# Attention probabilities that pass through HBM: four stores and two loads by key chunks in place of one store and four loads, and one product moved behind the others

## The chip, the cores and the metric

The kernel runs on one core of a Trainium2 chip. The metric is the device time of one execution in microseconds (us). TensorE (PE, with its weight loads PEld), VectorE (DVE), ScalarE (ACT) and GpSimd (POOL) each work through their own instruction list in order; SyncE (SP) issues the DMA transfers in order and waits, where an instruction must wait, at that place.

## The reference

Decayed causal attention over 32 heads (4 batches of 8), 576 queries and keys of width 64, then two dense layers of two matrices each over all 2304 tokens:

```python
scores = scale * np.matmul(q, k.transpose(0, 1, 3, 2))
decay = cum[:, :, :, None] - cum[:, :, None, :]
scores = np.where(causal, -1000000000.0, scores + decay)
attn = np.exp(scores - np.max(scores, axis=-1, keepdims=True))
attn = attn / (np.sum(attn, axis=-1, keepdims=True) + 1e-09)
out = np.matmul(attn, v)                  # per head
h = np.maximum(x @ w_in, 0.0); x = h * h @ w_out
h = x @ w_in2; out = (h - np.tanh(h)) @ w_out2
```

## The kernel before

Every product that needs fp32 accuracy is made from operands split into a rounded high part and a rest, so a product becomes two or three matmuls. PE makes the scores of a head (`s_ps`, L476 and L477), the value products (`o_ps`, L549, L552, L554), and in between the products of the first dense layer: twelve matmuls of 288 columns into `hp` (L138) and twelve into `yp` (L164) for each slice of the layer. The work of attention and of the dense layer is interleaved on PE so that one fills the waits of the other. Attention ends at about 550 us of 1080; behind it only dense work is left.

The softmax of a head is made with queries on the partitions, in five query tiles `t` (0 is the first 64 queries, 1 to 4 are 128 each). The value products need the probabilities with keys on the partitions. Heads 8 to 15 are turned by PE transposes (`trans`). Heads 16 to 31, which this change is about, go another way:

- `turn`: DVE transposes 32x32 blocks of the normalised probabilities `P` into the tile `T` (`PT["t"]`), after each query tile; the last of them is the one of t = 0 (L503).
- `put` (L512): one DMA of 1 MB stores `T` to the HBM scratch `p_d`, of which there are two, used in turn.
- `get` (L518): four DMAs load `p_d` into `PTl` (`PT["l"]`), one for each group of 32 partitions. There is one `PTl`, so the load of a head can't start before the value products of the head before it have read it.
- `split_p`: for each of four chunks of 128 keys, POOL makes the high part `PTh` (L90) and DVE the rest, in place in `PTl` (L101).
- `pv`: eight chunk products in the order high 0, high 1, rest 1, high 2, rest 2, high 3, rest 3, rest 0 (L552), the product of the last 64 keys (L549) ahead of the last of them, and `o0`, the product of the first 64 queries (L554), into a PSUM bank of its own. Its operand is the unsplit fourth chunk of `PTl`.

`attention_late` writes a head's steps down in the order scores, turns, `put(k)`, `pv(k-1)`, `get(k)`. Where each engine runs them is not this order: up to block 2 of the dense layer the order of a first build is kept (`MARK`), behind it a scheduler places every instruction by its own model of times. So a change of the transfers also moves instructions on all engines.

Of the kernel before, what the change touches and what calls it, by code (L numbers as in the profile page):

```python
# [9 lines left out]
F32 = mybir.dt.float32  # L10
# [43 lines left out]
def kernel(  # L54
# [10 lines left out]
    nc = tc.nc  # L65
# [8 lines left out]
    p_d = [dram.tile([128, 2048], F32, name=f"p_d{a}") for a in range(2)]  # L74
# [5 lines left out]
    def pre(u):  # L80
        return "" if u < UT else "l_"

    def by(name):
        return {"A": nc.scalar, "V": nc.vector, "P": nc.gpsimd, "S": nc.sync}[ENG[name]]

    def rounded(eng, out, in_):
        if eng is nc.scalar:
            eng.activation(out, in_, AF.Copy)  # L88
        elif eng is nc.gpsimd:
            eng.tensor_scalar(out, in_, 1.0, 1.0, ALU.mult, ALU.mult)  # L90
        else:
            eng.tensor_copy(out, in_)
# [83 lines left out]
    R, QA, QB, VR, VH, ST, XS, P, PT = {}, {}, {}, {}, {}, {}, {}, {}, {}  # L176

    def latest(engine):
        return next(x for x in reversed(nc.cur_bb.bb.instructions) if x.engine == engine)
# [249 lines left out]
    def store_x(b, pair, xs, c0, c1):  # L429
        STORED.add((b, pair, c1))  # L430
        n = c1 - c0
        xh = one.tile([128, S], F32R, tag="xsh", name="xsh")
        rounded(by(pre(b * H) + "xh"), xh[:, :n], xs[:, c0:c1])
        rest(by(pre(b * H) + "xl"), xs[:, c0:c1], xs[:, c0:c1], xh[:, :n])
        nc.sync.dma_start(x_d[b][pair][:, 0, c0:c1], xh[:, :n].bitcast(F32))
        nc.sync.dma_start(x_d[b][pair][:, 1, c0:c1], xs[:, c0:c1])
# [28 lines left out]
    def bank(u, name):  # L465
        return psa.tile([128, 512], F32, tag="at", name=name)
# [42 lines left out]
            nc.vector.transpose(T[:, 0:2, 2, 0], p[:, 512:576].rearrange("p (b j) -> p b j", b=2))  # L509

    def put(u):
        by("put").dma_start(p_d[u % 2], PT["t"].rearrange("p b a s j -> p (b a s j)"))  # L512

    def get(u):
        src = p_d[u % 2].rearrange("(q i) (b n) -> i q b n", q=4, b=4)
        for b in range(4):
            dst = PT["l"][32 * b:32 * b + 32].rearrange("p q a s j -> p q (a s j)")
            by("get").dma_start(dst.bitcast(F32), src[:, :, b])  # L518

    def split_p(a):  # L520
        hi, lo = PT["h"], PT["l"]
# [5 lines left out]
    def pv(u):  # L527
        vh, vr = VH.pop(u), VR.pop(u)
        b, h = divmod(u, H)
        e = h % 2  # L530
        ps = bank(u, "o_ps")
        if u < UT:
            hi, lo = (PT[k].rearrange("p q a s j -> p (q a s j)").rearrange("p (c t j) -> p c t j", c=4, t=4) for k in "hl")
            po = ps.rearrange("p (s j) -> p s j", s=4)
            at = lambda p, c, t: p[:, c, t:]
            po4, p4 = ps[0:64, 384:512].rearrange("p (q j) -> p q j", q=4), PT["t"][0:64, :, 3, 1]
            po_at = lambda t: po[:, t:]
            p0 = PT["t"][0:64, 2:4, 3, 0]
        else:
            hi, lo = PT["h"], PT["l"]  # L540
            po = ps.rearrange("p (q s j) -> p q s j", q=4, s=4)
            at = lambda p, c, t: p[:, :, c, t:]
            po4, p4 = po[0:64, :, 3], lo[0:64, :, 2, 0].bitcast(F32)
            po_at = lambda t: po[:, :, t:]
            p0 = lo[0:64, 0:2, 3, 0].bitcast(F32)
        seq = [(hi, 0), (hi, 1), (lo, 1), (hi, 2), (lo, 2), (hi, 3), (lo, 3), (None, 4), (lo, 0)]
        for n, (pt, c) in enumerate(seq):
            if pt is None:
                nc.tensor.matmul(po4, vr[0:64, 4], p4, start=False, stop=False)  # L549
                continue  # L550
            t = max(0, c - 1)
            nc.tensor.matmul(po_at(t), vh[:, c].rearrange("p a d -> p (a d)"), at(pt, c, t), start=(n == 0), stop=(n == 8))  # L552
        ps0 = bank(u, "o0_ps")
        nc.tensor.matmul(ps0[0:64, 0:64], vr[0:64, 0], p0, start=True, stop=True)  # L554
        if e == 0:
            XS[0] = two.tile([128, S], F32, tag="xs", name="xs")
        xs = XS[0]
        r = slice(64 * e, 64 * e + 64)
        xt = one.tile([64, 512], F32, tag="xsh", name="xt")
        rounded(nc.scalar, xt, ps[64:128])  # L560
        if u < UT:
            nc.vector.tensor_tensor(xs[r, 64:], ps[0:64], xt, ALU.add)
        else:
            nc.vector.tensor_tensor(
                xs[r, 64:].rearrange("p (s q j) -> p q s j", s=4, q=4),
                ps[0:64].rearrange("p (q s j) -> p q s j", q=4, s=4),
                xt.rearrange("p (q s j) -> p q s j", q=4, s=4), ALU.add,
            )
        rounded(by(pre(u) + "xs0"), xs[r, 0:64], ps0[0:64, 0:64])
        if e == 1:  # L570
            store_x(b, h // 2, xs, 0, S)
# [11 lines left out]
    def attention(u0):  # L583
        for p in range(u0 - 2, UT):
            if u0 - 1 <= p:
                load_v(p + 1)
            for t in (1, 4, 3, 2):
                if p >= u0:
                    trans(p, t)
                    yield  # L590
                if u0 <= p + 1:
                    scores(p + 1, t)
                    if t == 1:
                        scores(p + 1, 0)
                    elif p + 1 == UT:
                        turn(t)
                    yield
                if t == 4 and p + 2 < NU:
                    prep(p + 2)
                if t == 3 and p >= u0:  # L600
                    prep_v(p)
            if p + 3 < NU:
                load(p + 3)
            if p >= u0:
                pv(p)
            if p + 1 == UT:
                turn(1)
                turn(0)
                put(UT)
                get(UT)  # L610
            if p >= u0:
                yield

    def attention_late():
        for k in range(UT + 1, NU + 1):
# [25 lines left out]
            if now:  # L641
                turn(1)
                turn(0)
                put(k)
            pv(k - 1)
            yield
            if now:
                get(k)
# [120 lines left out]
    for g in range(len(BLK) * NF + LAG):  # L769
        j, i = divmod(g, NF)  # L770
        if (j, i) == MARK:
            first_part = {x.name for x in nc.cur_bb.bb.instructions}
        if j < len(BLK):
            ph, _, n = BLK[j]
# [23 lines left out]
        if jy >= 0:  # L798
            ph, tok, n = BLK[jy]
# [73 lines left out]
```

## Time and profile before

| | |
|---|---|
| median of 3 runs | 1085.09 us (1083.98 to 1085.87) |
| profiled execution, its own time | 1081.43 us |
| its span, first to last instruction | 1079.7 us |
| PE busy | 1029.2 us, 95% of the span |
| DVE, ACT, POOL busy | 594.0, 524.7, 250.6 us |
| DMA, mean rate over the span | 125 GB/s |

PE is the engine with the least idle time, so the end moves when PE's idle time or its clock does. Idle time of another engine counts only where PE waits for it.

### The profile page before, as it was taken

How to read it: one execution, taken by the hardware profiler on the slowest of the kernel's cores; microseconds unless marked ns; L12 is line 12 of the kernel's file. 1: busy time of each engine (PE TensorE's matmuls, PEld its weight loads, DVE VectorE, ACT ScalarE, POOL GpSimd, SP SyncE). 2: the span in 40 equal slices, each digit the busy share in tenths (PEclk: the TensorE clock that was granted, in tenths of full speed). 3: DMA queues.
4: the chain of work that ended last, by engine and by line, in shares of the span. 5: the costliest groups of instructions: out<-in, count | busy, mean ns of one | idle time of the engine just before them, and what ended most of it. 6: DMA issues, size and time to landing. Idle time of an engine off the chain costs nothing.

```text
span 1079.7 us, 16821 instructions
## 1 busy us (share of the span) xinstructions
PE 1029.2 (95%) x6048; PEld 898.8 (83%) x6048; DVE 594.0 (55%) x1566; ACT 524.7 (49%) x1221; POOL 250.6 (23%) x358
## 2 busy tenths in 40 slices
PE   4899999999999898999999999999999999999998
PEld 3577678888998888888889999888888888888898
DVE  5887777768787767877525545642222322222232
ACT  6977677665556446455436667432222222222232
POOL 4244455555353442534210000000000000000000
PEclk9989999999999899999989999999999999999999
DMA  7657643225955658745646088100200300110010
GB/s 243 199 138 213 185 140 136 89 82 174 293 180 171 195 154 253 258 141 162 184 161 228 2 305 285 45 1 25 92 1 1 117 1 1 39 40 1 1 40 21
DMA packets 63301, 134.83 MB, mean 125 GB/s; under 512 B 6416, under 2 KB 31568, under 8 KB 61168
## 3 DMA queue, kind: packets, MB, share of 16 engines
q1 hardware_dynamic: 63216, 133.74, 38.9%
q8 instruction: 48, 0.79, 0.3%
q14 instruction: 37, 0.30, 0.1%
HBM read 93.94 MB, written 39.78 MB: 124 GB/s over the span
## 4 chain that ended last, share of the span: by engine, by line
PE 75%; DMA 11%; DVE 6%; POOL 2%; issue 2%; SPq 2%; ACT 2%; POOLq 0%; ACTq 0%; DVEq 0%
PE hp L138 32%; PE yp L164 32%; DMA PTl<-p_d 6%; PE o_ps L552 3%; DMA p_d<-T 3%; PE o_ps L367 2%; DVE PTl L101 2%; PE s_ps L476 1%; SPq L518 1%; DVE P L443 1%; PE s_ps L477 1%; DMA raw<-in_w_dram 1%; POOL PTh L90 1%; PE s_ps L326 1%; PE t_ps L487 1%
## 5 line engine op out<-in xcount | busy, mean ns | idle before, releaser
L138 PE MATMUL hp<-xhl,w 128*128 128x288 f32 (+2 forms) x2496 | 454.2, 329 | 2.5 <-ACT tmp L148 1.7
L138 PEld LDWEIGHTS hp<-xhl,w 128*128 128x128 f32 x2496 | 388.8, 192 | 41.0 <-issue 2.7
L164 PE MATMUL yp<-ghl,w 128*128 128x512 f32 (+1 forms) x960 | 216.0, 374 | 0.0
L164 PE MATMUL yp<-gh,w 128*128 128x288 f32 x1024 | 200.9, 301 | 0.0
L164 PEld LDWEIGHTS yp<-ghl,w 128*128 128x128 f32 x960 | 168.4, 188 | 34.5
L153 DVE TENSOR_TENSOR tmp<-hp,tmp 128x512 f32<-128x512 f32 (+1 forms) x80 | 51.0, 638 | 209.8 <-ACT tmp L152 209.8
L164 PEld LDWEIGHTS yp<-gh,w 128*128 128x128 f32 x1024 | 161.9, 191 | 1.6 <-issue 0.4
L152 ACT ACTIVATE tmp<-hp 128x512 f32<-128x512 f32 (+1 forms) x80 | 44.4, 555 | 225.0 <-PE hp L138 224.8
L164 PE MATMUL yp<-gl,w 128*128 128x288 f32 x512 | 133.5, 299 | 2.6 <-DVE gl L101 1.5
L148 ACT ACTIVATE tmp<-hp 128x288 f32<-128x288 f32 x128 | 51.9, 407 | 121.6 <-PE hp L138 118.4
L452 ACT ACTIVATE P<-P,ST 128x320 f32<-128x320 f32 (+4 forms) x151 | 84.6, 561 | 39.5 <-DVE ST L443 38.2
L164 PEld LDWEIGHTS yp<-gl,w 128*128 128x128 f32 x512 | 90.4, 190 | 5.0 <-DVE gl L101 2.3
L463 POOL TENSOR_SCALAR P<-P,ST 128x448 f32<-128x448 f32 (+4 forms) x88 | 58.4, 666 | 93.3 <-DVE ST L457 52.3
L101 DVE TENSOR_TENSOR ghl<-tmp,ghl 128x512 fp32r<-128x512 f32 (+1 forms) x80 | 51.1, 639 | 49.2 <-ACT ghl L88 49.2
L443 DVE CUSTOM_DVE_ANT_0 P<-s_ps,mk 128x320 f32<-128x320 f32 (+3 forms) x151 | 63.6, 433 | 25.2 <-PE s_ps L477 12.0
L101 DVE TENSOR_TENSOR gl<-tmp,gh 128x288 fp32r<-128x288 f32 x96 | 48.4, 505 | 47.2 <-ACT tmp L150 46.6
L101 DVE TENSOR_TENSOR PTl<-PTl,PTh 128x512 fp32r<-128x512 f32 (+1 forms) x64 | 51.9, 841 | 39.4 <-POOL PTh L90 39.3
L88 ACT ACTIVATE ghl<-tmp 128x512 fp32r<-128x512 f32 (+1 forms) x80 | 47.2, 590 | 49.9 <-DVE tmp L153 49.8
L101 DVE TENSOR_TENSOR w<-wst,w 128x512 fp32r<-128x512 f32 x64 | 46.1, 725 | 28.9 <-ACT w L88 28.6
L90 POOL TENSOR_SCALAR PTh<-PTl 128x512 fp32r<-128x512 f32 (+1 forms) x64 | 46.3, 750 | 59.8 <-DMA PTl<-p_d 59.0
L149 ACT ACTIVATE gh<-tmp 128x288 fp32r<-128x288 f32 x128 | 56.5, 443 | 4.1 <-PE yp L164 1.2
L150 ACT ACTIVATE tmp<-tmp 128x288 f32<-128x288 f32 x128 | 56.0, 438 | 2.1
(122 smaller groups left out, 1187.7 us busy)
## 6 DMA issues: line engine op xcount, KB each, us to landing
raw<-in_w_dram SPq DMA_DIRECT2D x64, 512.0 KB
p_d<-T SPq DMA_DIRECT2D x16, 1024.0 KB
PTl<-p_d SPq DMA_DIRECT2D x64, 256.0 KB
R<-in_qk_dram SPq DMA_DIRECT2D x24, 576.0 KB
xhl<-y_d SPq DMA_DIRECT2D x16, 512.0 KB
xhl<-x_d SPq DMA_DIRECT2D x14, 576.0 KB
y_d<-yst SPq DMA_DIRECT2D x14, 576.0 KB
VR<-in_v_dram SPq DMA_DIRECT2D x32, 160.0 KB
```

The costliest lines, as they stand in the source:

```text
L88: eng.activation(out, in_, AF.Copy)
L90: eng.tensor_scalar(out, in_, 1.0, 1.0, ALU.mult, ALU.mult)
L101: eng.tensor_tensor(out, in_, hi.bitcast(F32), ALU.subtract)
L138: nc.tensor.matmul(ps, w[:, k * 128:(k + 1) * 128], xk, start=(jj == 0), stop=(jj == 11))
L148: nc.scalar.activation(tmp, ps, AF.Relu)
L149: nc.scalar.activation(gh, tmp, AF.Square)
L150: nc.scalar.activation(tmp, tmp, AF.Square)
L153: nc.vector.tensor_tensor(tmp, ps, tmp, ALU.subtract)
L164: nc.tensor.matmul(yp[m][:, :n], w[:, c], x, start=(i == 0 and j == 0), stop=(i == NF - 1 and j == 2))
L443: nc.vector.tensor_tensor_reduce(p[:rows, a:b], ps[:rows, :b - a], mk[:rows, o:o + b - a], -0.125, 3.0e38 if mn is None else mn, ALU.add, ...
L452: nc.scalar.activation(p[:rows, :n], p[:rows, :n], AF.Exp, bias=mn, scale=-1.0, accum_out=st[:rows, 1, t:t + 1])
L463: by(n_by).tensor_scalar(p[:rows, :n], p[:rows, :n], st[:rows, 3, t:t + 1], 1.0, ALU.mult, ALU.mult)
```

## The change

The one store becomes four, one for each group of 32 partitions of `T` (`q`), each with four runs of 512 values in a partition. The four loads become two; each fills all 128 partitions, the first with key chunks 0 and 1, the second with chunks 2 and 3, in runs of 256 values. The scratch in HBM keeps its layout. In `pv`, for all of heads 8 to 31, the product `o0` is tied behind the last chunk product on PE.

```diff
     def put(u):
-        by("put").dma_start(p_d[u % 2], PT["t"].rearrange("p b a s j -> p (b a s j)"))
+        dst = p_d[u % 2].rearrange("(b i) (q n) -> i q b n", b=4, q=4)
+        for q in range(4):
+            src = PT["t"][32 * q:32 * q + 32].rearrange("p b a s j -> p b (a s j)")
+            by("put").dma_start(dst[:, q], src)
 
     def get(u):
-        src = p_d[u % 2].rearrange("(q i) (b n) -> i q b n", q=4, b=4)
-        for b in range(4):
-            dst = PT["l"][32 * b:32 * b + 32].rearrange("p q a s j -> p q (a s j)")
-            by("get").dma_start(dst.bitcast(F32), src[:, :, b])
+        src = p_d[u % 2].rearrange("p (q a n) -> p q a n", q=4, a=4)
+        dst = PT["l"].rearrange("p q a s j -> p q a (s j)")
+        for a in (0, 2):
+            by("get").dma_start(dst[:, :, a:a + 2].bitcast(F32), src[:, :, a:a + 2])
...
         ps0 = bank(u, "o0_ps")
-        nc.tensor.matmul(ps0[0:64, 0:64], vr[0:64, 0], p0, start=True, stop=True)
+        with tc.issue_after(latest(EngineType.PE)):
+            nc.tensor.matmul(ps0[0:64, 0:64], vr[0:64, 0], p0, start=True, stop=True)
```

POOL's list at the high parts of head 25, with the semaphores that each instruction waits for (DMAHW0 to DMAHW7 are those of transfers). Before:

```order
L90 TENSOR_SCALAR PTh<-PTl 128x4x128 [waits DMAHW3_49,DMAHW2_49,DMAHW4_49,DMAHW1_49,Pool_49]
L90 TENSOR_SCALAR PTh<-PTl 128x4x128 [waits Pool_49]
L90 TENSOR_SCALAR PTh<-PTl 128x4x96 [waits Pool_49]
L90 TENSOR_SCALAR PTh<-PTl 128x4x64 [waits Pool_49]
L463 TENSOR_SCALAR P_1551<-P_1551,ST 128x448 [waits DVE_49,Activation_49]
```

And the same place in the changed kernel:

```order
L90 TENSOR_SCALAR PTh<-PTl 128x4x128 [waits DMAHW5_49]
L90 TENSOR_SCALAR PTh<-PTl 128x4x128
L463 TENSOR_SCALAR P_1551<-P_1551,ST 128x448 [waits DVE_49,Activation_49]
L90 TENSOR_SCALAR PTh<-PTl 128x4x96 [waits DMAHW6_49]
L90 TENSOR_SCALAR PTh<-PTl 128x4x64
```

The first two chunks wait for one transfer where they waited for four, the last two for another; a normalisation of the next head's scores (L463) may stand between.

PE's list from the last chunk product of head 24 (`o_ps<-PTl,VH 128x512`) onward, the first rows of it. Before:

```order
L552 MATMUL o_ps<-PTl,VH 128x512
L476 MATMUL s_ps<-QA 128x256
L477 MATMUL s_ps<-QB 128x256
L476 MATMUL s_ps<-QA 128x448
L477 MATMUL s_ps<-QB 128x448
L138 MATMUL hp<-xhl,w_0_455 128x288 x12
```

And in the changed kernel:

```order
L555 MATMUL o_ps<-PTl,VH 128x512
L558 MATMUL o_ps<-PTl,VR 64x64
L476 MATMUL s_ps<-QA 128x320
L477 MATMUL s_ps<-QB 128x320
L164 MATMUL yp<-gl,w_1_1698 128x288 x4
L138 MATMUL hp<-xhl,w_0_1878 128x288 x12
```

The product `o0` (64x64) now follows the last chunk product, and with it the first score product of head 26 (128x320) has moved behind the whole of `pv`; it stood between the chunk products. Up to the first chunk product of head 25 there are 64 products of 288 columns and thirteen others, where there were 40 and ten.

SP's list at the transfers of head 24. Before:

```order
L245 DMA VR<-in_v_dram 128x320
L512 DMA p_d_71<-T 128x2048
L435 DMA x_d_69<-xsh 128x576
L436 DMA x_d_69<-xs 128x576
L518 DMA PTl<-p_d_71 32x4x512 x4
```

And in the changed kernel:

```order
L515 DMA p_d_71<-T 32x4x512 x4
L245 DMA VR<-in_v_dram 128x320
L521 DMA PTl<-p_d_71 128x4x256 x2
L435 DMA x_d_69<-xsh 128x576
L436 DMA x_d_69<-xs 128x576
```

Four stores and two loads stand where one and four stood; the stores of `x_d` have moved behind the loads, and the load of `VR`, the values of a head, between.

## Rows read from the trace of the kernel before

**Rows 1.** The page: busy time, share of the span, and instructions by engine.

```profile
PE 1029.2 (95%) x6048; PEld 898.8 (83%) x6048; DVE 594.0 (55%) x1566; ACT 524.7 (49%) x1221; POOL 250.6 (23%) x358
```

**Rows 2.** Waits of PE from 250 to 560: waited for, total, times, longest.

```profile
PE o_ps L552 <- POOL PTh L90: 17.6, 9, 4.1
```

**Rows 3.** Timeline of PE: waiting first chunk products (start, length, [wait <-releaser]).

```profile
334.44 0.50 PE L552 MATMUL o_ps<-PTh,VH 128*128 128x512 f32 x1 [2.17 <-POOL PTh L90]
...
355.87 0.80 PE L552 MATMUL o_ps<-PTh,VH 128*128 128x512 f32 x1 [4.08 <-POOL PTh L90]
...
393.64 0.49 PE L552 MATMUL o_ps<-PTh,VH 128*128 128x512 f32 x1 [1.73 <-POOL PTh L90]
...
432.17 0.50 PE L552 MATMUL o_ps<-PTh,VH 128*128 128x512 f32 x1 [1.70 <-POOL PTh L90]
...
455.05 0.49 PE L552 MATMUL o_ps<-PTh,VH 128*128 128x512 f32 x1 [1.35 <-POOL PTh L90]
...
507.35 0.50 PE L552 MATMUL o_ps<-PTh,VH 128*128 128x512 f32 x1 [1.80 <-POOL PTh L90]
...
541.96 0.79 PE L552 MATMUL o_ps<-PTh,VH 128*128 128x512 f32 x1 [3.79 <-POOL PTh L90]
```

**Rows 4.** Windows at half clock: stretch, length, busy time (instructions) by engine, granted clock.

```profile
core 0: us, PE busy (x) PEld busy (x) DVE busy (x) ACT busy (x) POOL busy (x), PEclk, DMA share, GB/s
...
335.40:338.80 3.40, 3.40 (x15) 3.31 (x15) 3.40 (x8) 0.00 (x0) 3.40 (x4) 0.50 0.01 2
...
355.90:362.70 6.80, 6.80 (x26) 6.21 (x27) 6.74 (x10) 0.00 (x0) 5.84 (x6) 0.50 0.17 58
...
471.90:475.30 3.40, 3.40 (x14) 3.30 (x14) 3.34 (x11) 0.44 (x2) 2.79 (x5) 0.50 0.00 0
...
540.20:547.00 6.80, 5.04 (x18) 4.40 (x19) 3.58 (x6) 0.60 (x2) 2.91 (x4) 0.50 0.00 1
```

**Rows 5.** Chain that ended last: start, length, what.

```profile
342.12 5.49 DMA p_d<-T
...
403.01 3.88 DMA p_d<-T
...
423.33 0.43 PE o_ps L552
...
425.18 6.15 DMA PTl<-p_d
...
431.50 0.63 POOL PTh L90
...
440.87 4.89 DMA p_d<-T
...
447.13 7.00 DMA PTl<-p_d
...
456.29 1.59 PE hp L138 x12
```

**Rows 6.** Windows by transfer rate: last two columns are DMA share and GB/s.

```profile
8.30:9.30 1.00, 0.52 (x3) 0.38 (x2) 1.00 (x5) 0.93 (x2) 0.61 (x1) 1.00 0.91 319
403.80:406.40 2.60, 2.48 (x19) 2.31 (x18) 1.80 (x7) 2.42 (x7) 1.14 (x1) 1.00 1.00 409
...
424.90:430.70 5.80, 5.57 (x43) 5.34 (x41) 5.73 (x22) 5.74 (x17) 1.32 (x2) 1.00 0.94 224
432.00:433.25 1.25, 1.08 (x6) 0.77 (x7) 1.10 (x2) 0.20 (x1) 1.25 (x3) 1.00 1.07 370
```

**Rows 7.** Timeline of SP (lengths are issue times): first stores, head 26.

```profile
7.16 0.79 SPq L184 DMA_DIRECT2D aug_d<-chl  x2
...
440.87 0.33 SPq L512 DMA_DIRECT2D p_d<-T  x1
...
445.82 1.74 SPq L518 DMA_DIRECT2D PTl<-p_d  x4
```

**Rows 8.** The instructions of line 554: shortest, median, longest ns, first and last start.

```profile
L554 PE MATMUL o_ps<-PTl,VR x32: 218/267/366, 268.3 to 542.8; 64*64 64x64 f32 x32
```

## The prediction, made before the changed kernel ran

> **What bounds the kernel now.** I read the page first. PE is busy for 95% of the span [rows 1], so time can be won only where PE waits or runs at a low clock. Behind 550 us only dense work is left, which the order leaves nearly as it was; the change lies between 250 and 550 us, where heads 16 to 31 pass. There I read PE's waits: its first chunk products wait for POOL's high parts nine times, 17.6 us in all [rows 2]. That is the largest wait by far, and the one the change can reach. The windows add the second cost: in four stretches of together 20.4 us the granted clock is 0.50, the lower of its two levels (1.2 against 2.4 GHz), and PE is busy in 18.64 us of them [rows 4]. Three of the four follow a first chunk product that waited 2.17, 4.08 or 3.79 us [rows 3]. Work done at half clock costs its time twice, so about 9.3 us are lost there. Waits and clock together make 27 us; more than that isn't to be had from this path.
>
> The chain of waits says what is late. At head 25 the last chunk product of head 24 ends at 423.76, the loads are issued at once, the last of them takes 6.15 us to land, and POOL starts at 431.50. At head 26 the store is issued at 440.87 and lands after 4.89 us, the last load takes 7.00 us from 447.13, and PE goes on about 0.7 us after POOL starts at 454.38 [rows 3, 5]. So two kinds of head wait: where the load is held up by the products of the head before (1.73, 1.70, 1.80 us at 393, 432 and 507), and where the store comes late (2.17, 4.08, 1.35, 3.79 us at 334, 355, 455 and 541) [rows 3]. The first sum to 5.2 us, the second to 11.4 us; two short ones make up the 1.0 us to 17.6.
>
> **The load.** Issue of all four loads takes 1.74 us [rows 7], and the last needs 6.15 to 7.00 us from its own issue [rows 5], so with three issues (1.3 us) ahead of it and 0.2 us to POOL's start the load costs 7.6 to 8.5 us; I take 7.8. The reason is its rate: 224 GB/s at a busy share of 0.94, where a load that fills 128 partitions in runs of 1152 bytes (`xhl` from `x_d`) gets 370 and the store 409 GB/s [rows 6]. After the change POOL waits for the first half alone, 0.52 MB into 128 partitions in runs of 1 KB. Its fixed part I take from the store: 3.88 us [rows 5] less 1.05 MB at 409 GB/s (2.6 us) is 1.3 us. With 1.4 us for the data at 370 GB/s and 0.2 us to POOL's start that is 2.9 us; at the old load's 224 GB/s it would be 3.8. I take 3.4, for the load of `VR` now stands just ahead on the queue in some heads. The load thus falls from 7.8 to 3.4 us.
>
> **The store.** No store of `T` in four pieces is in the trace. Lower end: the two stores of `chl` at 7.16 us go from 32 partitions too [rows 7], and while they run the engines move 319 GB/s [rows 6]; 1.05 MB at that rate are 3.3 us, with the fixed part 4.6 us. Upper end: the old load is the same pattern with source and destination exchanged; if the stores are as slow, they take 7.6 us. Four issues of 0.33 us [rows 7] lie under the data either way. The stores now take 3.9 to 5.5 us [rows 5], some 0.7 us over the best where other transfers share the engines. I take the lower end with that 0.7, 5.3 us, since it is nearest to what is changed: a store from 32 partitions. Old store and load: 4.6 + 7.8 = 12.4 us. New: 5.3 + 3.4 = 8.7 us, 3.7 us less.
>
> A rule of the Trainium skill speaks against this choice: the page "SBUF — State Buffer", section "Door 1: The DMA port swizzle", says that a transfer's bandwidth depends on how many of 16 ports its partitions reach, and 32 partitions reach half of them. The old load's 224 GB/s agrees with half of the page's 435, the 319 GB/s of the early stores doesn't. By the page the store's data would take 4.8 us, the store 6.1 before any interference.
>
> **What the order gives back.** The scheduler reckons with the new transfers and sets PE's list anew, so a shorter chain isn't all gain. I count PE's work in its list, 1.59 us per twelve products of 288 columns [rows 5] and the score products at some 0.15 us each. Between the last chunk product of one head and the first of the next, the five shortest gaps held 6.4 to 7.6 us, at heads 23, 25, 27, 29 and 31; head 25 had 40 products of 288 columns and ten others, 6.5 us. Now the shortest is 5.5 us, the next 8.4, and head 25 has 64 and thirteen, 10 us. The new load needs 0.2 us to be issued, 3.4 to POOL's start and 0.7 us to PE, 4.3 us. It fits in every gap, so the waits of the first kind (5.2 us, and the 1.0) go. The store-bound heads have less room: from a head's last score product to its first chunk product the five tightest heads held 14.5, 17.6, 18.1, 18.4 and 18.6 us of PE work, 17.4 on average, and now hold 14.4, 14.5, 14.9, 15.1 and 15.9, 15.0 on average. Of the 3.7 us the order has spent 2.4. The tight heads keep 1.3 us each, 6.5 us over five, and 5 of the 11.4 us of waiting are left.
>
> **The rest.** The second half lands up to 2 us behind the first; POOL and DVE are then still at the first two chunks, and the order puts dense products between in the heads that are tight. I set 1 us for what shows. Moving `o0` (0.27 us on PE, [rows 8]) costs nothing by itself: the same number of products. The next head's first score product moves back with it, covered because its second one must wait for `o_ps` to be evicted anyway; without that cover 2 to 5 us would be added to a store-bound head. In SP's list stores and loads issue in 2.2 us where it was 2.1. One head has a load of 0.59 MB between its stores, 1.4 us at 409 GB/s.
>
> **The sum.** Waits: 17.6 - 5 - 1 = 11.6 us won. Clock: the longest waits shrink to under 3 us, so I count half of the 9.3 us, 4.6 won. Together 16.2 us. The profiled execution takes 1081.43 us, so 1065.2 of its own; it lies 3.7 us under the median of the runs, 1085.09, and on the median the forecast is **1069 us**, with a range of its own from 1063 to 1075.
>
> **The rivals.** A change within 0.2%, 2.2 us, is about what a measurement of this kernel can't tell from none.
>
> - *The stores are slow* (the other side). At 7.6 us the chain is 11.0, 1.4 shorter, and the room 2.4 shorter: five tight heads wait 1 us more each, and the next five (17 to 19 us of room) begin to, 3 us. 11.4 + 5 + 3 + 1 = 20.4 us of waits against 17.6, and with longer waits some 2 us more at half clock: 1090. It decides from a store of about 7 us. For it: the load's rate, and the page. Against it: 319 GB/s.
> - *DVE is next.* Between the landing at 431.33 and the store at 440.87 lie 9.5 us [rows 5] in which DVE splits, evicts and turns in one list. If that list sets the store's time, the store-bound heads keep their 11.4 us, and only 5 to 6 us go, with 1 to 2 of the clock: 1078.
> - *The order takes it all back.* Room shrinks as much as the chain and the first kind's gain turns into waits within `pv`: 1085. For it: 2.4 of 3.7 are gone in the count.
> - *Nothing waits.* With the early stores' rate, little interference and PE never idle long enough for the clock to fall: 17.6 + 9.3, 1058.
>
> **How the numbers follow.** Forecast 0.42, nothing waits 0.16, DVE next 0.15, order takes all 0.09, slow stores 0.18. The first three are faster, 0.73; same 0.09; slower 0.18. The range from 1057 to 1089 leaves out the far end of the slow stores and a little below.
>
> **What would show it.** Right: four stores landing in about 5 us; POOL starting 3 to 4 us after the first load's issue; waits of the first chunk products in sum under 7 us, and one or no half-clock stretch. Wrong: a store of 7 us or more, at a rate near 224 GB/s; POOL late for another reason than its transfer; new waits at the third chunk's product.

## The result, and the profile after

The changed kernel takes 1095.82 us (median of 4 runs, 1094.66 to 1096.11); the kernel before took 1084.53 beside it (4 runs, 1082.82 to 1085.87). The ratio is 1.010 with a 95% interval from 1.0079 to 1.0121: 11 us slower, where I had forecast 1069 and a range up to 1089. The profiled execution spans 1094.2 us, 14.5 more than that of before, which had come out 3 us under the median. Set beside each other by the products into `hp`, the two traces are 1.5 us apart at 257 us and stay 14.5 us apart from 577 us on, so nearly the whole loss lies between, where the change is.

Two sentences ahead have to be corrected. The scratch in HBM does not keep its layout: the exchange of rows and columns of 32x32 blocks has moved from the load to the store. And the turn of t = 0 isn't always the last one before a head's store: in the trace of before it is so in 11 of the 16 heads, in that of after in 4.

The page after, engines:

```profile
PE 1037.6 (95%) x6048; PEld 901.1 (82%) x6048; DVE 589.1 (54%) x1566; ACT 525.8 (48%) x1221; POOL 244.7 (22%) x358
```

The waits of PE after, from 250 to 560 us (waited for, total, times, longest; L555 is the old L552, L558 the old L554):

```profile
PE o_ps L555 <- POOL PTh L90: 8.5, 7, 2.0
PE o_ps L555 <- DVE PTl L101: 4.1, 5, 1.7
PE yp L164 <- DVE gl L101: 4.0, 5, 1.4
PE yp L164 <- DVE yst L101: 2.2, 3, 1.2
PE s_ps L476 <- DVE xs L92: 2.2, 2, 1.6
PE s_ps L476 <- DVE ST L443: 2.0, 2, 1.4
PE o_ps L555 <- DVE ST L457: 1.5, 1, 1.5
```

The wait for POOL has halved, from 17.6 [rows 2] to 8.5 us. But every other row shown waits for DVE: 16.0 us in the six rows, 17.2 with two short ones behind them, where the same view of before has 4.5 us for DVE:

```profile
PE s_ps L476 <- DVE xs L92: 1.6, 1, 1.6
PE yp L164 <- DVE gl L101: 1.5, 1, 1.5
PE o_ps L552 <- DVE ST L456: 0.8, 1, 0.8
PE o_ps L552 <- DVE PTl L101: 0.6, 1, 0.6
```

The waits of DVE after, same stretch:

```profile
DVE xs L92 <- PE o_ps L558: 11.8, 9, 1.9
DVE T L506 <- DMA p_d<-T: 6.4, 5, 1.9
```

Neither row stood in this view of before. DVE now stands nine times at the eviction of `o0`, and five times its turns wait until the stores have read the last head out of `T`.

Windows of after: the six stretches at half clock, then two in which a head's four stores run, then one of a head's loads (stretch, length, busy time by engine, granted clock, DMA share, GB/s):

```profile
257.94:261.35 3.41, 3.41 (x16) 3.39 (x16) 2.10 (x9) 1.52 (x4) 2.16 (x3) 0.50 0.70 229
275.01:278.42 3.41, 3.41 (x13) 2.40 (x12) 1.79 (x5) 0.85 (x2) 0.00 (x0) 0.50 1.05 388
326.21:329.62 3.41, 2.90 (x11) 2.80 (x12) 3.35 (x6) 0.44 (x1) 3.41 (x4) 0.50 0.92 254
391.06:397.89 6.83, 6.73 (x24) 5.62 (x25) 6.36 (x27) 2.85 (x9) 2.00 (x4) 0.50 0.34 110
445.68:452.51 6.83, 6.48 (x25) 5.78 (x24) 6.77 (x15) 2.06 (x7) 4.26 (x6) 0.50 0.81 261
486.64:490.05 3.41, 3.27 (x14) 3.27 (x15) 3.27 (x15) 3.19 (x10) 0.92 (x2) 0.50 0.00 0
413.35:418.23 4.88, 4.88 (x33) 4.23 (x33) 2.17 (x6) 2.41 (x6) 0.74 (x1) 1.00 0.97 229
435.54:440.23 4.69, 4.69 (x36) 4.66 (x35) 3.80 (x15) 3.63 (x10) 0.00 (x0) 1.00 0.93 223
420.18:425.06 4.88, 4.88 (x38) 4.88 (x37) 2.00 (x5) 3.91 (x11) 1.24 (x3) 1.00 0.92 318
```

Half clock rose from 20.4 us [rows 4] to 27.3. PE is busy in 26.2 of them, so it loses 13.1 us there where it lost 9.3. The stores run at 223 to 229 GB/s with the DMA engines busy, where the one store had 409 [rows 6]; the loads got faster, 318 against 224. Only the 223 belongs to the stores alone; in the other windows, those of before too, SP had issued a load of `VR` or transfers of `x_d` or `y_d` as well.

SP after, at the transfers of one head (start, issue time), and the chain of waits through the same head:

```profile
412.54 2.78 SPq L515 DMA_DIRECT2D p_d<-T  x4
416.28 0.35 SPq L245 DMA_DIRECT2D VR<-in_v_dram  x1
418.82 1.20 SPq L521 DMA_DIRECT2D PTl<-p_d  x2
420.12 1.50 SPq L435 DMA_DIRECT2D x_d<-xsh  x1
```

```profile
414.09 4.65 DMA p_d<-T
...
418.82 4.63 DMA PTl<-p_d
...
423.54 0.63 POOL PTh L90
```

First store to first load: 6.3 us. First load to POOL: 4.7 us. In SP's and POOL's timelines of heads 19 to 31 these two are 5.7 to 7.2 us, median 6.1 (but for head 20 with 11.0, two of whose stores SP issued only behind a load of `R`), and 3.7 to 5.6 us, median 3.9. So the chain is some 10.0 us where I had reckoned 12.4 before and forecast 8.7.

### The profile page after: what moved, and what is told of

It is laid out like the page before. It is cut to its first block, busy times and chain, and to the rows that moved or that the text cites. A ratio compares the mean times of both kernels' runs of the same rounds, so it can differ in the third digit from the quotient of the medians.

```text
span 1094.2 us, 16838 instructions
## 1 busy us (share of the span) xinstructions
PE 1037.6 (95%) x6048; PEld 901.1 (82%) x6048; DVE 589.1 (54%) x1566; ACT 525.8 (48%) x1221; POOL 244.7 (22%) x358
## 4 chain that ended last, share of the span: by engine, by line
PE 67%; DVE 11%; DMA 11%; issue 5%; POOL 2%; ACT 2%; SPq 1%; DVEq 0%; ACTq 0%; POOLq 0%
PE hp L138 29%; PE yp L164 29%; DMA p_d<-T 4%; DMA PTl<-p_d 4%; PE o_ps L555 2%; PE o_ps L367 2%; DVE PTl L101 2%; DVE T L506 2%; DVE P L443 2%; DMA raw<-in_w_dram 1%; DVE QA L101 1%; POOL PTh L90 1%; DVE P L463 1%; DVE gl L101 1%; PE s_ps L476 1%
## 5 line engine op out<-in xcount | busy, mean ns | idle before, releaser
L164 PE MATMUL yp<-gh,w 128*128 128x288 f32 x1024 | 197.5, 300 | 2.2 <-DVE yst L101 2.2
L164 PEld LDWEIGHTS yp<-gh,w 128*128 128x128 f32 x1024 | 159.6, 190 | 4.6 <-DVE yst L101 3.0
L164 PE MATMUL yp<-gl,w 128*128 128x288 f32 x512 | 129.9, 301 | 6.1 <-DVE gl L101 4.0
L463 POOL TENSOR_SCALAR P<-P,ST 128x448 f32<-128x448 f32 (+4 forms) x88 | 60.7, 693 | 102.2 <-DVE ST L457 59.2
L101 DVE TENSOR_TENSOR PTl<-PTl,PTh 128x512 fp32r<-128x512 f32 (+1 forms) x64 | 47.1, 751 | 33.9 <-POOL PTh L90 33.9
L101 DVE TENSOR_TENSOR w<-wst,w 128x512 fp32r<-128x512 f32 x64 | 46.9, 737 | 27.4 <-ACT w L88 27.3
L90 POOL TENSOR_SCALAR PTh<-PTl 128x512 fp32r<-128x512 f32 (+1 forms) x64 | 38.5, 618 | 76.8 <-DMA PTl<-p_d 74.2
```

The source lines that it names most:

```text
L101: eng.tensor_tensor(out, in_, hi.bitcast(F32), ALU.subtract)
L164: nc.tensor.matmul(yp[m][:, :n], w[:, c], x, start=(i == 0 and j == 0), stop=(i == NF - 1 and j == 2))
L463: by(n_by).tensor_scalar(p[:rows, :n], p[:rows, :n], st[:rows, 3, t:t + 1], 1.0, ALU.mult, ALU.mult)
```

## The experiments

Two theories at first. **A**: the lists lose, that is, the order that the scheduler makes for the new transfers together with the tie of `o0`. **B**: the transfers lose, the slow stores above all. They are told apart by giving one kernel the lists of another. "In the lists of before" means that every engine's list is that of before word for word, with the new transfers where the old ones stood. `other` is the order made with the transfers and `o0` of before, and it binds every instruction:

```diff
-    nc = build(True, [i.name for f in first.m.functions for bb in f.blocks for i in bb.instructions])
+    other = names(build(True, names(build(False, []).m)).m)
...
+    nc = build(True, [n for a in other for n in to.get(a, [])], True)
```

"Own lists" are those that the scheduler makes for the kernel itself.

**The transfers alone, own lists** (the diff without its last hunk, `o0` free):

> The four stores and two loads of the change; the product of the first 64 queries is free again, and the scheduler makes its own lists. Theory A (the lists cost it: with the product tied behind, DVE's eviction of it and the next head's scores come late): most of the 11 us are gone, 1087 us or less. Theory B (the transfers cost it: a store takes 6.2 us where it took 4.6, and the tile T is held longer): as slow as the changed kernel, 1092 us or more, with store plus first load near 10 us as there.

Measured: 1088.98 us, 1.002 (1.0002 to 1.0038).

**The tie alone, own lists** (the last hunk of the diff alone):

> The one store and four loads of before; only the product of the first 64 queries is tied behind the chunk products, with lists of the scheduler's own. Theory A: slower than before by 5 us or more, 1090 us up, with DVE waiting for that product some 10 us in all. Theory B: within 3 us of before, 1081 to 1088.

Measured: 1096.14 us, 1.009 (1.0065 to 1.0115). The tie with the old transfers, in the lists that come with it, costs as much as the whole change.

**The new transfers in the lists of before** (`o0` free):

> The four stores and two loads, but every engine keeps the list of the kernel before word for word (in SP's list each store or load group stands where the old one stood). So only the transfers differ. Theory A: faster than before, 1080 us or less: the chain store plus load is 2.3 us shorter, less what the product of the first 64 queries waits for the second load, about 1 us a head where PE has no slack. Theory B: slower than before, 1088 us or more.

Measured: 1075.25 us, 0.9895 (0.9856 to 0.9935): 11 us faster than before. Its PE waits from 250 to 560 (L593 is the old L552, L596 the old L554):

```profile
PE yp L171 <- DVE gl L108: 9.0, 4, 5.6
PE o_ps L596 <- DMA PTl<-p_d: 3.7, 4, 1.5
...
PE o_ps L593 <- POOL PTh L97: 0.8, 1, 0.8
```

The first chunk products hardly wait any more, 0.8 against 17.6 us, slow stores and all. What is left is DVE, and `o0`, whose operand comes with the second load. The transfers alone with own lists have these (L577 is the old L552, L580 the old L554):

```profile
PE o_ps L577 <- POOL PTh L91: 8.4, 7, 2.2
PE o_ps L580 <- DMA PTl<-p_d: 6.3, 5, 2.5
```

Same transfers, same `o0`, another list: 8.4 us of waits for POOL against 0.8, 27.3 us at half clock against 17.1, and 14 us more in all.

**The old transfers in the lists of after**:

> The one store and four loads, in the lists of the changed kernel word for word. Theory A: the lists alone cost more than 10 us, and the chain is 2.3 us longer than they were made for: 1096 us or more. Theory B: faster than the changed kernel, 1090 us or less.

Measured: 1119.7 us, 1.0314 (1.028 to 1.0349). In a given list the new transfers win 11 us (before's) or 24 us (after's). B falls, A stands.

Next: what in the lists loses? **Theory 1**, DVE stands at the eviction of `o0`. **Theory 2**, the tie takes the next head's score products out of the chunk products, and all heads fall into one pace. **Theory 3**, any list that isn't that of before loses.

**The tie, with ACT evicting `o0`** (old transfers, own lists):

```diff
-    "l_xs0": "V"
+    "l_xs0": "A"
```

> One store and four loads as before and the product o0 tied behind the last chunk product, as in the run of the tie alone (1096.1 us, 1.009 of before); here ACT instead of DVE evicts o0's bank in the late heads. In that run DVE waited 10.8 us, eight times, for o0, and the waits of the first chunk products for POOL were 20.4 us. Theory 1, the tie costs because DVE stands at this eviction with the next head's turns behind it: DVE's wait for o0 goes, and most of the 10 us of loss with it, 1085 to 1089. Theory 2, the tie costs because the next head's score products lose their places between the chunk products, so that all heads go at one pace and each waits for its own store: the loss stays, 1093 to 1099, with 18 to 24 us of waits for POOL. Theory 3, any list that isn't the one of before loses some 10 us: 1093 to 1099 too; the two runs with a slightly changed pace tell 2 and 3 apart.

Measured: 1092.27 us, 1.0072 (1.0043 to 1.0102); 1.009 with DVE. DVE's wait at `o0` is gone, most of the price isn't, so theory 1's forecast is missed. But the list is a new one again, and the next two runs show what that alone can do: theory 1 is weakened, not refuted.

**Two other paces, nothing else changed** (own lists; they set where attention is laid among the dense work):

```diff
-CUT = (25, 44, 61, 2)
+CUT = (26, 44, 61, 2)
```

```diff
-ENDS = (28, 27, 27, 27, 32, 24)
+ENDS = (28, 27, 27, 28, 32, 24)
```

> Transfers and o0 as before; one number of the pace at which attention is laid among the dense work (CUT, 25 to 26) is changed, which moves some 70 of 1880 rows in PE's list and the tight rooms little (five tightest from last score product to first chunk product 17.8 us on average, 17.4 before). Theory 3, the list of before is a lucky one and any other loses: 1091 to 1098. Theories 1 and 2, the loss belongs to the tie: within 3 us of before, 1083 to 1090.

Measured: 1088.57 us, 1.0024 (1.0 to 1.0049).

> As the run before this one with another number of the pace (ENDS, 27 to 28 for the fourth part), which moves some 120 rows of PE's list; five tightest rooms 17.4 us on average, as before. Theory 3: 1091 to 1098. Theories 1 and 2: 1083 to 1090.

Measured: 1099.45 us, 1.013 (1.0086 to 1.0173). A step of one in one number of the pace can cost as much as the whole change under study. Its PE waits:

```profile
PE o_ps L577 <- POOL PTh L91: 25.0, 11, 3.9
```

Neither theory expected that spread: a list by itself is worth 0.2% or 1.3%. So the tie's 0.9% has to be measured at several paces.

**The changed kernel at the two paces** (both diffs together with the change):

> The changed kernel whole (four stores, two loads, o0 tied), laid out at the first of the two other paces (CUT 26), in the lists that the scheduler then makes. With the old transfers and o0 free that pace cost 0.2%, the second 1.3%. Theory 3, the loss is the list that fell out and not what was changed: with another list the changed kernel moves by as much, and here the tight rooms are wider (15.7 us on average, 15.0 in the changed kernel, five of them 16.0 and 14.5): 1080 to 1092, some way towards the 1075 of the new transfers in the lists of before. Theory 2, the tie sets one pace for all heads whatever the list: 1093 to 1099 as the changed kernel.

Measured: 1094.81 us, 1.0084 (1.0056 to 1.0112).

> The changed kernel at the second other pace (ENDS 28). Tight rooms 14.9 us on average, as in the changed kernel. Theory 3: anywhere from 1085 to 1108, and not within 3 us of the run before this one. Theory 2: 1093 to 1099.

Measured: 1098.18 us, 1.012 (1.0084 to 1.0156). The changed kernel is slow at all three paces, 1094.8 to 1098.2, as theory 2 forecast. Theory 3 missed the first of the two runs (1080 to 1092); the second, 3.4 us from the first, fits it as well.

**The tie alone and the transfers alone at the two paces**:

> Old transfers, o0 tied, at the first other pace (o0 free there: 1.0024 of before). Theory 2, the tie costs by itself: some 0.9% above that, 1.009 to 1.014. Theory 3, any list that isn't the one of before: 0.997 to 1.013, no nearer to one end.

Measured: 1091.4 us, 1.0051 (1.0029 to 1.0074).

> Old transfers, o0 tied, at the second other pace (o0 free there: 1.0130 of before). Theory 2: 1.018 to 1.024. Theory 3: 1.000 to 1.013, so not slower than with o0 free; its tight rooms are the wider ones (18.3 us on average against 17.4).

Measured: 1091.69 us, 1.0055 (1.0035 to 1.0074), less than with `o0` free. Both runs fall to theory 3.

> New transfers, o0 free, at the first other pace, own lists (with o0 tied there: 1.0084 of before; at the pace of before 1.002). Theory 2: 0.997 to 1.003, below the tied one. Theory 3: 0.997 to 1.012. With the transfers' 1% gain alone, had the list cost nothing more than it did with the old transfers, it would be 0.992.

Measured: 1088.73 us, 1.0025 (1.0007 to 1.0042).

> New transfers, o0 free, at the second other pace, own lists (with o0 tied there: 1.0120 of before). Theory 2: 1.000 to 1.006. Theory 3: 0.997 to 1.014. The transfers' gain alone on that pace's 1.0130 would give 1.003.

Measured: 1084.55 us, 0.9992 (0.9971 to 1.0013). Both theories allow the first of these two runs, theory 3 alone the second, which lies just under theory 2's range.

The twelve together, own lists, as ratios to before, and behind them the five tightest rooms (PE's work in its list from a head's last score product to its first chunk product, mean in us):

| | pace of before | pace a | pace b | rooms |
|---|---|---|---|---|
| old transfers, `o0` free | 1 | 1.0024 | 1.0130 | 17.4, 17.8, 17.4 |
| old transfers, tied | 1.0090 | 1.0051 | 1.0055 | 18.0, 18.6, 18.3 |
| new transfers, `o0` free | 1.0020 | 1.0025 | 0.9992 | 15.8, 16.1, 15.8 |
| new transfers, tied | 1.0100 | 1.0084 | 1.0120 | 15.0, 15.7, 14.9 |

With the new transfers the tie costs 0.8, 0.6 and 1.3%: at each pace, as theory 2 has it, though three paces are few beside a spread of 1.3%. With the old ones it costs 0.9 and 0.3% and gains 0.7%: no effect that stands out of the spread of lists, which is theory 3. And the new transfers, worth 1% in the lists of before, are worth +0.2, 0.0 and -1.4% in the scheduler's own.

**Why the stores are slow**, old loads, `o0` free, in the lists of before. Four stores of 32 partitions, 8 KB in one piece from each:

```diff
+for q in range(4):
+    by("put").dma_start(p_d[u % 2][32 * q:32 * q + 32], PT["t"][32 * q:32 * q + 32].rearrange("p b a s j -> p (b a s j)"))
```

> Everything as before, in the lists of before, but the one store of T is cut into four of 32 partitions each, which write the scratch in the old layout, 8 KB in one piece from each partition. It asks why the four new stores take some 6.2 us instead of 4.6. Theory S, it is the 32 partitions of one transfer: 6 us or more from the store's issue to the load's, and 1 to 1.5 us more wait in some four store-bound heads, 1087 to 1094. Theory D, it is the destination in 2 KB pieces: the store stays at 4 to 5 us and the time within 3 us of before.

Measured: 1105.87 us, 1.0185 (1.0155 to 1.0215). And four stores from all partitions, to pieces of 2 KB at a pitch of 8 KB:

```diff
+for b in range(4):
+    by("put").dma_start(p_d[u % 2][:, 512 * b:512 * b + 512], PT["t"][:, b].rearrange("p a s j -> p (a s j)"))
```

> As the run before this one, but cut along the rows: four stores from all 128 partitions, each 2 KB from a partition to a destination in 2 KB pieces at a pitch of 8 KB. Theory S: the store stays at 4 to 5 us, time within 3 us of before. Theory D: 6 us or more, 1087 to 1094.

Measured: 1080.91 us, 0.995 (0.9927 to 0.9972). SP's rows at a head's store and load and a window of each run, first the groups of 32 partitions, then the cut by columns:

```profile
310.76 2.69 SPq L533 DMA_DIRECT2D p_d<-T  x4
...
317.00 1.75 SPq L548 DMA_DIRECT2D PTl<-p_d  x4
312.30:316.80 4.50, 4.50 (x34) 4.42 (x34) 2.46 (x9) 3.74 (x10) 0.74 (x1) 1.00 0.88 216
```

```profile
308.98 1.79 SPq L536 DMA_DIRECT2D p_d<-T  x4
...
311.47 2.41 SPq L548 DMA_DIRECT2D PTl<-p_d  x4
310.40:313.50 3.10, 3.10 (x23) 3.02 (x23) 2.31 (x9) 2.54 (x7) 0.74 (x1) 1.00 1.01 334
```

Theory S holds: 32 partitions at a time make the store slow, even with 8 KB in one piece; the scattered destination doesn't. In the first run a head's loads are issued 6.2 us after its first store. In the second the first load no longer waits for all four stores, and the last load is out 4.9 us after the first store. Windows of the first run show 216 to 249 GB/s; of the second 295 to 369, and in one 224 with the engines 0.70 busy, but there loads run beside the stores. The price was under-forecast: mostly 6.1 to 7.1 us from store to load, and 20 us in all, not 1 to 8. By columns the time came out 2 us below what was expected: first store to first load takes mostly 2.5 to 4.3 us where it was 3.9 to 5.6. Load `b` reads only what store `b` wrote, so it needn't wait for all four; that this is the cause is argued from the code. Little of it reaches POOL: from the first load to POOL's start heads 19 to 31 take 8.5 us (median) where before had 7.6, so that from the first store on it is 12.8 against 13.0.

**Eight loads**: the one store of before, four loads for key chunks 0 and 1, then four for 2 and 3, in the lists of before:

```diff
-src = p_d[u % 2].rearrange("(q i) (b n) -> i q b n", q=4, b=4)
-for b in range(4):
-    dst = PT["l"][32 * b:32 * b + 32].rearrange("p q a s j -> p q (a s j)")
-    by("get").dma_start(dst.bitcast(F32), src[:, :, b])
+src = p_d[u % 2].rearrange("(q i) (b a n) -> i q b a n", q=4, b=4, a=4)
+for a in (0, 2):
+    for b in range(4):
+        dst = PT["l"][32 * b:32 * b + 32].rearrange("p q a s j -> p q a (s j)")
+        by("get").dma_start(dst[:, :, a:a + 2].bitcast(F32), src[:, :, b, a:a + 2])
```

> One store as before; eight loads, four for key chunks 0 and 1 and then four for chunks 2 and 3, each into 32 partitions; o0 not tied; every engine's list that of before, word for word but for the transfers. It asks which half of the new transfers won the 11 us of the run with the new transfers in the lists of before (1075.2). Theory P, waiting for the first half of the load is what wins, and the slower store was a loss: POOL starts 5 to 6 us after the first load's issue (half the data at 224 GB/s is 2.3 us, four issues 1.7 us, some 1.5 us fixed) and the store stays at 4 to 5 us, a chain of about 10 us, as with the new transfers: 1073 to 1078. Theory Q, the loads into 128 partitions are what wins, since halves into 32 partitions share one rate and eight issues take 3.5 us: POOL starts 6.5 us or more after, and the time is 1080 to 1086.

Measured: 1061.69 us, 0.9793 (0.9757 to 0.983), 22.5 us faster than before (1084.22 beside it) and better than either theory had it. Its PE waits from 250 to 560:

```profile
PE yp L171 <- DVE gl L108: 3.6, 2, 2.5
PE hp L145 <- ACT tmp L155: 2.2, 3, 1.2
PE s_ps L483 <- DVE xs L99: 1.6, 1, 1.6
PE o_ps L593 <- POOL PTh L97: 1.3, 1, 1.3
```

POOL starts mostly 4.5 to 5.8 us after the first load's issue, the store is as before, and between 250 and 600 us one stretch of 3.4 us is left at half clock. Waiting for half the load is what wins; that the slow stores were a loss in the changed transfers follows from the run of the groups of 32 partitions, where they cost 20 us.

**The eight loads in own lists**:

> One store and eight half loads, o0 free, in the lists that the scheduler makes for them. In the lists of before these transfers gave 1061.7 us, 0.979, with hardly a wait left (5 us of waits of the first chunk products' kind and none at half clock but one). If the own lists spend what a shorter chain gives, as theory 2 and 3 both have it for the changed transfers (lost there: 14 us of 11): 1070 to 1082. If it was only the slow store that couldn't be paid: 1060 to 1066.

Measured: 1077.13 us, 0.9924 (0.9902 to 0.9945); the wait for POOL is back:

```profile
PE o_ps L577 <- POOL PTh L91: 6.9, 5, 2.4
```

By the two ratios 1.3%, 14 us of the 22.5, are lost to the list, as the changed transfers lost 14.

**Stores by columns and eight loads, in the lists of before**:

> Four stores by columns from all partitions and eight half loads, in the lists of before. The stores by columns took some 1.3 us less than the one store from issue to the next load, and gave 0.5% with the old loads. With half loads hardly a first chunk product waits any more, so little is left to win: 1057 to 1063. If eight loads behind four stores collide on the queue, the load grows past 6 us and the time is 1064 to 1070.

Measured: 1066.9 us, the median of four runs from 1057.11 to 1074.77; the ratio, without the longest, is 0.9796 (0.9721 to 0.9871). It can't be told from the eight loads alone.

## Why the prediction was wrong

**What bounds the kernel: right.** The path of 27 us is there to be had: eight loads in the lists of before win 22.5 of it, by the waits and stretches that I had named. One reading was loose: the last of the four stretches at half clock begins at 540.20, in the wait of 3.79 us and 1.8 us ahead of the product that it is said to follow [rows 3, 4].

**The load: right in kind, a little short.** 3.4 us forecast, between 2.9 and 3.8; a median of 3.9 measured.

**The store: mis-sized.** 5.3 us forecast, a median of 6.1 measured; the upper end was 7.6. The choice of the lower end rested on the 319 GB/s that ran beside the stores of `chl` [rows 6, 7]. SP's timeline of before has a row just behind them:

```profile
7.16 0.79 SPq L184 DMA_DIRECT2D aug_d<-chl  x2
7.99 1.32 SPq L184 DMA_DIRECT2D R<-in_qk_dram  x2
```

Loads of `R` were issued 0.8 us behind them, and the two stores are 0.29 MB in all, where the window of 8.30 to 9.30 us alone moved 0.32 MB: it holds bytes of those loads. It was no row on stores from 32 partitions alone. By the rule of the Trainium skill that I had set aside ("SBUF — State Buffer", "Door 1: The DMA port swizzle": 32 partitions reach half of the ports) my estimate had been 6.1 us. The trace agrees: 223 GB/s for the four stores alone.

Still, the store alone didn't make the kernel slower: with it the transfers win 11 us in the lists of before. The rival of the slow stores had the side right, and not the whole cause. It has a share: one store and eight half loads take 1.0% less than the four stores and two loads, both in the lists of before (0.9793 against 0.9895) and in own lists (0.9924 against 1.0020), though the loads differ there too.

**"Moving `o0` costs nothing by itself": this step failed.** I called the move of the next head's score product covered, because its second product waits for the eviction of `o_ps` anyway, and priced the lack of cover at 2 to 5 us for a store-bound head. The tie costs 0.6 to 1.3%, 6 to 14 us, with the new transfers at each of three paces. What in it costs is only partly shown. In after, DVE stands 11.8 us at `o0`'s eviction, and 17.2 us of PE's waits are for DVE, where the transfers alone have 7.6; but the trial with ACT at that eviction, made with the old transfers, won nothing that can be measured. At the other two paces the tie shows in another wait: PE's waits for POOL are 18.4 and 15.2 us with it, 8.4 and 8.8 without.

**"What the order gives back": this step failed too, in size.** I had counted room shrinking by 2.4 us against 3.7 us of shorter chain and let the tight heads keep 1.3 us each. The chain became 2.4 us shorter, so by the same count nothing was left, which is the rival "the order takes it all back". But the count reached only one wait. A new list moves every engine's work: one number of the pace, with the rooms unchanged, cost 1.3%, 14 us. The lists with the tie have one thing in common: a head's store is issued later after its scores. Head 25 shows it, rows of PE, DVE and SP put in order of time, in before and with the tie alone:

```profile
406.49 0.28 PE L477 MATMUL s_ps<-QB 68*128 68x64 f32 x1
...
413.11 0.24 DVE L503 STREAM_TRANSPOSE T<-P 64x64 f32<-64x64 f32 x1
...
413.37 0.34 SPq L512 DMA_DIRECT2D p_d<-T  x1
...
416.01 1.09 DVE L101 TENSOR_TENSOR PTl<-PTl,PTh 128x512 fp32r<-128x512 f32 x1 [2.67 <-POOL PTh L90]
```

```profile
416.12 0.27 PE L478 MATMUL s_ps<-QB 68*128 68x64 f32 x1
...
423.38 1.09 DVE L102 TENSOR_TENSOR PTl<-PTl,PTh 128x512 fp32r<-128x512 f32 x1 [3.89 <-POOL PTh L91]
...
425.15 3.31 DVE L102 TENSOR_TENSOR PTl<-PTl,PTh 128x512 fp32r<-128x512 f32 x3
...
428.91 0.23 DVE L504 STREAM_TRANSPOSE T<-P 64x64 f32<-64x64 f32 x1
...
429.16 0.33 SPq L514 DMA_DIRECT2D p_d<-T  x1
```

Before, the last turn stands on DVE ahead of the splits of head 24, and the store is issued 6.9 us after the last score product. With the tie DVE waits 3.89 us for head 24's load, splits it, and turns last; the store comes after 13.0 us. The last turn stands behind the other head's splits in 8 of 15 heads in before and in 13 with the tie alone. There heads 19 to 29 all take 11.0 to 14.4 us from score to store, where before four of them took 5.1 to 6.9: the one pace of theory 2. The changed kernel hasn't that pace (4.9 to 14.5 us). The mean of this time over heads 16 to 31, in us:

| | pace of before | pace a | pace b |
|---|---|---|---|
| old transfers, `o0` free | 9.7 | 10.6 | 10.8 |
| old transfers, tied | 11.4 | 10.9 | 11.0 |
| new transfers, `o0` free | 8.6 | 8.5 | 9.0 |
| new transfers, tied | 9.8 | 10.8 | 10.3 |

The tie lengthens it in all six pairs, by 1.2 to 2.2 us with the new transfers. With the old ones it rises with the loss from 9.7 us to 11.4 (the tie with ACT has 11.1), but pace b with `o0` free, which loses most, has 10.8. So it is at most a part, and that it is the cause is argued and not shown.

**The sum.** Waits for POOL: 11.6 us forecast won, 9.1 measured. Clock: 4.6 forecast won, 3.8 lost. Not in the sum: 12.7 us of further waits for DVE (17.2 less 4.5). In all PE's idle time grew by 6.1 us (span less busy: 56.6 against 50.5 [rows 1]) and its busy time by 8.4, of which the clock explains 3.8; the other 4.6 I can't put to a row.

**DVE next**, the rival with 0.15, named the right engine with a price on the wrong side: I had it hold up the stores alone, and not PE.

**What stays open.** Which of the tie's effects costs the 0.6 to 1.3% with the new transfers: DVE's stand at `o0`, or the later stores. What in an own list costs the 1.3% at pace b isn't known either. The tie within otherwise unchanged lists was not tried, since the score products that stand between the chunk products would have to move with it.

## What to carry to other kernels

When a scheduler sets the order, a change has two prices, that of the work and that of the new lists; the second can be larger, so time the new work once in the old lists and the old work at a few settings of the scheduler before you believe either. A load on which a chain waits is best split by what is needed first, not by partitions; and a store cut into groups of 32 partitions was slow here (6.2 us to the first load), one cut by columns wasn't (4.9 us to the last). A rate read from a window belongs to a transfer only if nothing else was issued beside it.

## What was not expected of the hardware

Four stores of 256 KB from 32 partitions each, one behind the other on one queue, ran at 223 GB/s while the DMA engines showed 0.93 busy: a busy engine isn't an engine at its rate. Four stores from all partitions with 2 KB pieces, loads beside them, had 334 GB/s at 1.01. Eight loads into 32 partitions, issued in 4 to 5 us, brought the first half to POOL mostly 4.5 to 5.8 us after the first issue.
